# P kept in fp32 for 7 of 16 groups of the filter stages, and the order of the steps where they end

## The chip, the cores and the metric

The kernel runs on one core of a Trainium2 chip. The metric is device time in microseconds (us) of one execution. A core has five engines with instruction queues of their own: PE (TensorE, the matmul array, whose weight loads the profile shows as PEld), DVE (VectorE), ACT (ScalarE), POOL (GpSimd) and SP (SyncE, which here only issues DMAs).

## The reference

Four layers on x of 2048 tokens by 640 channels: a spectral filter, a token mixer, and the same two again.

```python
def _A_ref(x, w_r, w_i):
    X = jnp.fft.rfft2(x, axes=(-2, -1))
    X = X * (w_r + 1j * w_i)
    return jnp.fft.irfft2(X, (S, D), axes=(-2, -1))

def _B_ref(x, w1, b1, w2, b2):
    h = _layernorm(x, axis=-1)
    u = _gelu(jnp.einsum("bsd,sf->bdf", h, w1) + b1)
    y = jnp.einsum("bdf,fs->bds", u, w2) + b2
    return y.transpose(0, 2, 1)

x = A_x
x = x + _A_ref(_layernorm(x, axis=-1), A_w_r, A_w_i)
x = x + _B_ref(_layernorm(x, axis=-1), B_w1, B_b1, B_w2, B_b2)
x = x + _A_ref(_layernorm(x, axis=-1), A_w_r, A_w_i)
x = x + _B_ref(_layernorm(x, axis=-1), B_w1, B_b1, B_w2, B_b2)
```

## The kernel before

The Fourier transforms are done as matrix products with tables. Nearly every operand of a product is held as two fp16 numbers, a high part and the remainder (names in h and l), and a product is three matmuls: high by high, high by low, low by high.

A filter layer has three parts. A first one transforms the tokens of each of 16 tiles (s1h, s1l). The second one, `a1`, is what the change is about and is called the filter stage here: it goes over 16 groups of rows of the spectrum. The third, `a2`, transforms back over the channels (products of Y with the table tDi), copies the result out as eh and el, transforms over the tokens (products with tIM) and adds to x. The first filter stage lies at 59.3 to 119.8 us of the profile, the second at 536.9 to 599.1.

The steps of one group in `a1`, with the names of the schedule:

- d: PE multiplies s1h, s1l and a stack of leftovers (stk) with the table tD; the result P lies in PSUM.
- ph: ACT copies P, scaled, into fp16 (ph). pl: DVE takes P minus ph into fp16 (pl).
- sA and sB: PE multiplies P with the table tS2, in two halves. The array is used as four quadrants of 64x64; a half is 12 matmuls, three rounds over the quadrants. The second half waits for an ACT instruction that is itself tied to the end of the first half (marked `&` in the schedule; for group 0 it is DVE's small copy `between`).
- ta and tb: DVE multiplies the result with the filter weights w. sa and sb: POOL adds and subtracts them.
- xh, xl, uh, ul: ACT and POOL split the product into fp16 parts, and ACT repeats some columns.
- i: PE transforms back (tI2). Yh, Yl: ACT and DVE copy the result out in two fp16 parts.

Four PSUM slots are shared by the steps (`@` gives the slot). The order of all steps is written out by hand in `STEPS`, one string for each of the two filter stages, and each engine keeps it. Steps that begin with e belong to neighbouring work: ea4 to ea7 are ACT's part of splitting the first weight tile of the mixer (`wsplit`, four pieces of wh), ev10 is DVE's computing of the scale cxe that eh needs, ev4 DVE's computing of the scale s that the weight pieces need. They stand at the end of the first stage's string.

```python
for op in STEPS[not first].split():
    if op[0] == "e":
        scale(op)
        continue
    do(op)
```

In `a2`, iteration i does the product of Y for tile i (`id_mm`), then el and the tIM product of tile i - 1, and near its end eh of tile i.

Of the kernel before, what the change touches and what calls it, by code (L numbers as in the profile page):

```python
# [59 lines left out]
TS = 4096.0  # L60
# [30 lines left out]
class Layers:  # L91
# [226 lines left out]
    def a0_open(self, first=False):  # L318
        nc, A = self.nc, self.A
        p = self.pS1 = self.push("S1", side=self.sp)  # L320
        self.s1h = p.tile([128, 80, 2, 16, 4], F16, name=f"s1h{self.n}")
        self.s1l = p.tile([128, 80, 2, 16, 4], F16, name=f"s1l{self.n}")
        self.tD = p.tile([128, 20, 161], F16, name=f"tD{self.n}")
        self.tS2 = p.tile([128, 2, 2, 4, 128], F16, name=f"tS2{self.n}")
        self.tI2 = p.tile([128, 2, 2, 2, 128], F16, name=f"tI2{self.n}")
        p = self.pT = self.push("a0", side=self.sp)
        if first:
            self.tM = [p.tile([128, 4, 128], F32, name=f"tM{q}_{self.n}") for q in range(4)]
        else:
            self.tM = [p.tile([128, 4, 2, 128], F16, name=f"tM{q}_{self.n}") for q in range(4)]  # L330
# [149 lines left out]
    def a1(self, first):  # L480
# [190 lines left out]
        ps = dstage(0, slots[0])  # L671
        if not first:
            self.wsplit(0, (0,), hi=False)
        pp[0] = tuple(self.t(p, [128, 2, 322], F16, a, 3) for a in ("ph", "pl"))
        sc = PQS / (S1S * TS)
        for q in range(2):
            a, b, c = ps[:, q, :NL], pp[0][0][:, q, :NL], pp[0][1][:, q, :NL]
            T.activation(b, a, AF.Copy, scale=sc)
            V.scalar_tensor_tensor(c, a, sc, b, op0=ALU.mult, op1=ALU.subtract)

        def acted(ins, gs):

            for g in map(int, gs.split(",") if gs else ()):
                follow(ins, half[g])
                half[g] = ins

        def do(op):
# [101 lines left out]
    def a2(self, li):  # L789
# [69 lines left out]
        for i in range(NJ + 5):  # L859
# [1266 lines left out]
def _shape_tables():  # L2126
# [66 lines left out]
```

## Time and profile before

| | |
|---|---|
| median of 3 runs | 976.7 us (975.47 to 977.51) |
| the profiled execution | 974.83 us, of which its span from first to last instruction is 973.1 us |
| PE busy | 932.0 us, 96% of the span |
| DVE busy | 754.3 us, 78% |
| ACT busy | 564.6 us, 58% |
| POOL busy | 293.4 us, 30% |
| chain that ended last | PE 55%, DVE 21%, ACT 8%, POOL 7% |

The profile is of one execution. Busy shares are over the whole span; the mixer stages, which fill most of it, keep PE at work with the other engines partly idle, and the filter stages are short. Ends of matmuls are modelled and overlap each other, so PE's busy time is not time at its peak. The chain that ended last is followed back from the last instruction to what released each step.

### The profile page before, as it was taken

How to read it: one execution, taken by the hardware profiler on the slowest of the kernel's cores; microseconds unless marked ns; L12 is line 12 of the kernel's file. 1: busy time of each engine (PE TensorE's matmuls, PEld its weight loads, DVE VectorE, ACT ScalarE, POOL GpSimd, SP SyncE). 2: the span in 40 equal slices, each digit the busy share in tenths (PEclk: the TensorE clock that was granted, in tenths of full speed). 3: DMA queues.
4: the chain of work that ended last, by engine and by line, in shares of the span. 5: the costliest groups of instructions: out<-in, count | busy, mean ns of one | idle time of the engine just before them, and what ended most of it. 6: DMA issues, size and time to landing. Idle time of an engine off the chain costs nothing.

```text
span 973.1 us, 22470 instructions
## 1 busy us (share of the span) xinstructions
PE 932.0 (96%) x9009; PEld 691.0 (71%) x9009; DVE 754.3 (78%) x1407; ACT 564.6 (58%) x869; POOL 293.4 (30%) x496
## 2 busy tenths in 40 slices
PE   4889899999999999999999998999999999999998
PEld 3768777677767677677776776776777777777776
DVE  7989989999788956566667897889645445998885
ACT  5857869885667774455544476784433335455431
POOL 6949867311111112222222595771000000000000
PEclk9999999999999999999999999999999999999999
DMA  7856377654876776664232663764555447655411
GB/s 254 290 159 175 107 235 243 224 174 161 317 272 228 278 251 205 229 187 130 97 108 74 192 183 104 247 221 162 169 156 170 142 132 289 205 189 177 139 52 49
DMA packets 68108, 179.42 MB, mean 184 GB/s; under 512 B 8010, under 2 KB 15332, under 8 KB 68004
## 3 DMA queue, kind: packets, MB, share of 16 engines
q1 hardware_dynamic: 60820, 151.63, 48.5%
q0 software_dynamic: 7184, 26.36, 7.4%
q8 instruction: 70, 1.15, 0.5%
q14 instruction: 34, 0.28, 0.1%
HBM read 130.39 MB, written 47.58 MB: 183 GB/s over the span
## 4 chain that ended last, share of the span: by engine, by line
PE 55%; DVE 21%; ACT 8%; POOL 7%; issue 5%; DMA 3%; SPq 0%; ACTq 0%; DVEq 0%; POOLq 0%
PE ps L83 55%; DVE f L83 4%; DVE wl L83 3%; POOL eo L83 3%; DVE st L83 3%; DVE s1l L83 2%; ACT wh L83 2%; ACT z L83 1%; DMA xt<-x 1%; ACT junk L83 1%; DVE xt L83 1%; DVE Yl L83 1%; POOL xl L83 1%; POOL ta L83 1%; DVE tb L83 1%
## 5 line engine op out<-in xcount | busy, mean ns | idle before, releaser
L83 PEld LDWEIGHTS <-wh 128*128 128x128 f16 x2298 | 222.4, 98 | 88.8 <-issue 2.1
L83 PE MATMUL ps<-u,wh 128*128 128x320 f16 x1242 | 228.6, 299 | 0.0
L83 PEld LDWEIGHTS <-wl 128*128 128x128 f16 x1626 | 158.8, 98 | 66.0 <-DVE wl L83 3.0
L83 PE MATMUL ps<-u,wl 128*128 128x320 f16 x826 | 182.1, 299 | 1.0 <-DVE wl L83 0.5
L83 PEld LDWEIGHTS <-wo 128*128 128x128 f16 x924 | 90.3, 98 | 35.1
L83 POOL TENSOR_TENSOR r<-v,mh 128x1 f32<-128x1 f32 x64 | 39.4, 615 | 148.0 <-DVE nm L83 138.4
L83 PE MATMUL ps<-tDi,Yh 128*128 128x322 f16 x320 | 71.3, 300 | 1.5 <-ACT Yh L83 1.5
L83 DVE TENSOR_TENSOR f<-eo 128x256 f32<-128x256 f32 (+1 forms) x124 | 39.1, 368 | 37.0 <-POOL eo L83 36.3
L83 ACT ACTIVATE junk<-raw 128x896 bf16<-128x896 f32 (+1 forms) x60 | 59.5, 991 | 13.3 <-DMA raw<-w 12.5
L83 POOL TENSOR_TENSOR xt<-xt,ec 128x320 f32<-128x320 f32 x64 | 53.3, 853 | 29.9 <-DVE xt L83 29.8
L83 ACT ACTIVATE z<-xt,nb,r 128x640 f32<-128x640 f32 x31 | 28.5, 919 | 54.2 <-POOL z L83 45.1
L83 DVE BATCH_NORM_STATS2 st<-xt 128x6 f32<-128x320 f32 x126 | 55.2, 479 | 5.2 <-DMA xt<-x 4.6
L83 PE MATMUL ps<-u,wo 128*128 128x320 f16 x420 | 58.8, 299 | 0.0
L83 PE MATMUL ps<-tM,f 128*128 128x128 f32 x160 | 39.1, 419 | 19.4 <-DVE f L83 19.4
L83 POOL TENSOR_TENSOR eo<-z 128x320 f32<-128x320 f32 x60 | 52.3, 892 | 17.0 <-ACT z L83 15.2
L83 PE MATMUL ps<-tDi,Yl 128*128 128x322 f16 x192 | 55.7, 299 | 1.4 <-DVE Yl L83 1.4
L83 DVE SCALAR_TENSOR_TENSOR wl<-raw,s,wh 128x896 f16<-128x896 f32 (+2 forms) x43 | 47.9, 1122 | 7.3 <-ACT wh L83 7.3
L83 PEld LDWEIGHTS ps<-tM,f 128*128 128x128 f32 x160 | 33.4, 300 | 24.9 <-DVE f L83 24.5
L83 POOL TENSOR_TENSOR xl<-ta,xh 128x642 f16<-128x642 f32 (+2 forms) x34 | 45.5, 1346 | 5.0 <-ACT xh L83 4.9
L83 ACT ACTIVATE wh<-raw,s 128x896 f16<-128x896 f32 (+2 forms) x46 | 43.6, 987 | 3.1 <-DVE s L83 1.8
L83 DVE SCALAR_TENSOR_TENSOR u<-f,su,u 128x1280 f16<-128x1280 f32 (+2 forms) x26 | 25.5, 996 | 25.4 <-ACT u L83 25.2
L83 POOL MEMSET wl<- 64x256 f16 x2 | 0.6, 306 | 146.5 <-DMA wl<-w2A 146.5
(257 smaller groups left out, 2237.6 us busy)
## 6 DMA issues: line engine op xcount, KB each, us to landing
xt<-x SPq DMA_DIRECT2D x79, 320.0 KB
raw<-w SPq DMA_DIRECT2D x32, 512.0 KB
w<-w SPq DMA_DIRECT2D x48, 321.0 KB
x<-xt SPq DMA_DIRECT2D x47, 320.0 KB
raw<-w SPq DMA_DIRECT2D x32, 448.0 KB
raw<-w2z SPq DMA_DIRECT2D x32, 448.0 KB
out<-xt SPq DMA_DIRECT2D x15, 320.0 KB
w1S<-wl POOLq DMA_DIRECT2D x9, 512.0 KB, 6.4
```

The lines of the kernel that those rows point to most:

```text
L83: i = f(*a, **k)
```

## The change

For groups 0, 1, 2, 12, 13, 14 and 15 (`WHOLE`), in both filter stages, P is copied by ACT into one fp32 tile pf, and no pl is made. The two s halves of such a group multiply pf with a new fp32 table tS1, four matmuls a half instead of twelve. tS1 (1024 fp32 numbers a partition) is loaded with the other tables. In the first stage's string, ev10 comes ahead of ev4, and ea4 to ea7 go; ACT's four wh pieces are issued in `a2` instead, one behind eh of each of the tiles 0 to 3. In the second stage's string some of the last steps change places (Yl7 comes earlier, and the second half of group 15 is tied to xh13 instead of ul12).

```diff
 STEPS = '''
-    Yh14 Yl12 xl15b i15a@0 uh15 ul15 Yl14 i15b@3 Yh15a Yh15b Yl15a Yl15b ev4 ev10 ea4 ea5 ea6 ea7
+    Yh14 Yl12 xl15b i15a@0 uh15 ul15 Yl14 i15b@3 Yh15a Yh15b Yl15a Yl15b ev10 ev4
...
-    sB14 pl15 sa13 i9@1 xh12 ta14 ul10 sb13 uh12 i8@3 Yh7 tb14 xl12 Yh9 sb14 sA15@0 xh13 sa14 Yl9 uh13 ul12&15 xl13
-    xh14 sB15 Yl7 ul11 i10@1 uh14 Yh8 ta15a xl14 i11@2 tb15a Yh10 ta15b ul13 sa15a tb15b ul14 Yl8 Yh11 i13@0 sb15a
+    sB14 sa13 i9@1 xh12 ta14 ul10 sb13 uh12 i8@3 Yh7 tb14 Yl7 xl12 sA15@0 xh13&15 Yh9 sb14 uh13 sa14 Yl9 ul12 xl13
+    xh14 sB15 ul11 i10@1 uh14 Yh8 ta15a xl14 i11@2 tb15a Yh10 ta15b ul13 sa15a tb15b ul14 Yl8 Yh11 i13@0 sb15a
...
+WHOLE = 0, 1, 2, 12, 13, 14, 15
...
+        self.tS1 = p.tile([128, 2, 4, 128], F32, name=f"tS1{self.n}")
...
         nc.sync.dma_start(self.tI2, A["tI2"])
+        nc.sync.dma_start(self.tS1, A["tS1"])
...
-        def psplit(ps):
+        def psplit(ps, g):
+            sc = PQS / (S1S * TS)
+            if g in WHOLE:
+                pf = self.t(p, [128, 2, 322], F32, "pf", 3)
+                yield T.activation(pf[:, :, :NL], ps[:, :, :NL], AF.Copy, scale=sc)
+                yield pf
...
         def s2half(g, ps, x, half):
 
             out = []
+            if g in WHOLE:
+                for R, C in ((0, 0), (0, 1), (1, 1), (1, 0)):
+                    ri, q = R ^ half, R ^ C
+                    out.append(mm(
+                        ps[HALF[C], ri, :NL], self.tS1[HALF[R], 1 if g == 0 else 0, 2 * ri + q, HALF[C]], x[HALF[R], q, :NL],
+                        start=half == 0, stop=half == 1,
+                    ))
+                return out[0], out[-1]
...
             if has[0]:
                 eo[i] = ehigh(pd[i])
+                if first and i < 4:
+                    c = i ^ 2
+                    self.wsplit(0, (c // 2,), lo=False, part=slice(c % 2 * 4, c % 2 * 4 + 4))
```

What this moves on the engines is seen best in the order of their instructions (names carry buffer numbers, which differ between the two kernels). On PE, at the first groups of the first stage, the rows before are these, from the small product of eye and xb to the first matmul with pl; each matmul has a weight load of its own.

```order
L83 MATMUL ps_908<-eye,xb 128x16
L83 LDWEIGHTS tS_197
L83 MATMUL ps_908<-ph_1026,tS_197 64x321
L83 LDWEIGHTS tS_197
...
L83 LDWEIGHTS tS_197
L83 MATMUL ps_908<-pl_1027,tS_197 64x321
```

And these are the rows of the change at that place, with group 0's eight matmuls ahead of it, up to the next d block; fp32 matmuls load their weights themselves, without a row.

```order
L84 MATMUL ps_909<-pf_967,tS_199 64x321 x8
L84 MATMUL ps_910<-eye,xb 128x16
L84 MATMUL ps_910<-pf_1025,tS_199 64x321 x4
L84 LDWEIGHTS s1h_194
L84 MATMUL ps_911<-tD_196,s1h_194 64x160
```

Twelve weight loads and twelve matmuls have become four rows of pf. On DVE, at the same place, before:

```order
L83 SCALAR_TENSOR_TENSOR pl_966<-ps_907,ph_965 128x321 x2
L83 COPY between_911<-between_911 128x1
L83 TENSOR_REDUCE xm<-ps_908 16x1
L83 COPY xb<-xm 16x128
L83 SCALAR_TENSOR_TENSOR pl_1027<-ps_908,ph_1026 128x2x321
L83 TENSOR_SCALAR xqq<-ps_908 128x16
```

and in the change:

```order
L84 COPY between_913<-between_913 128x1
L84 TENSOR_REDUCE xm<-ps_910 16x1
L84 COPY xb<-xm 16x128
L84 TENSOR_SCALAR xqq<-ps_910 128x16
L84 TENSOR_SCALAR qi_232_1053<-xqq 128x16
```

The rows of pl are gone and nothing took their place. On ACT, at the seam between the first filter stage and `a2`, the rows before, behind the last Yh:

```order
L83 ACTIVATE wh_1346<-raw_1342,s_72 128x512 x2
L83 ACTIVATE wh_1346<-raw_1344,s_72 128x512 x2
L83 ACTIVATE eh_2878<-ps_2861,cxe 128x644
L83 ACTIVATE eh_2906<-ps_2880,cxe 128x644
L83 ACTIVATE ec_2937<-ps_2899 128x322
```

and in the change:

```order
L84 ACTIVATE eh_2749<-ps_2732,cxe 128x644
L84 ACTIVATE wh_1293<-raw_1291,s_72 128x512
L84 ACTIVATE eh_2778<-ps_2752,cxe 128x644
L84 ACTIVATE wh_1293<-raw_1291,s_72 128x512
L84 ACTIVATE ec_2810<-ps_2771 128x322
L84 ACTIVATE eh_2818<-ps_2784,cxe 128x644
L84 ACTIVATE wh_1293<-raw_1289,s_72 128x512
```

The four pieces of wh have moved from ahead of the first eh to places behind each of the first four.

## Rows read from the trace of the kernel before

**Rows 1.** Windows, both filter stages: from:to length, busy us (instructions), PEclk, DMA, GB/s

```profile
core 0: us, PE busy (x) PEld busy (x) DVE busy (x) ACT busy (x) POOL busy (x), PEclk, DMA share, GB/s
59.30:119.80 60.50, 56.30 (x1511) 46.47 (x1511) 54.72 (x93) 43.80 (x91) 49.03 (x59) 1.00 0.51 148
536.90:599.10 62.20, 55.90 (x1507) 45.88 (x1508) 55.96 (x89) 41.26 (x84) 49.32 (x64) 1.00 0.63 187
```

**Rows 2.** Waits of PE, first filter stage: us in total, times, longest us

```profile
PE ps L83 <- DVE Yl L83: 1.0, 2, 0.6
PE ps L83 <- DVE pl L83: 0.9, 2, 0.6
PE ps L83 <- DVE ta L83: 0.6, 2, 0.4
PE ps L83 <- DVE between L83: 0.3, 1, 0.3
PE ps L83 <- DVE tb L83: 0.2, 1, 0.2
```

**Rows 3.** Waits of PE, second filter stage

```profile
PE ps L83 <- ACT xl L83: 1.7, 1, 1.7
PE ps L83 <- DVE Yl L83: 1.5, 2, 1.2
...
PE ps L83 <- DVE pl L83: 0.7, 2, 0.4
```

**Rows 4.** Groups of instructions by shape, DVE, first filter stage

```profile
L83 DVE SCALAR_TENSOR_TENSOR Yl<-ps,Yh 128x384 f16<-128x384 f32 x30 | 14.7, 544 | 0.0
L83 DVE SCALAR_TENSOR_TENSOR ta<-ps,sx,w 128x642 f32<-128x642 f32 x15 | 13.2, 879 | 0.9 <-issue 0.4 <-POOL xl L83 0.3 <-PE ps L83 0.2
L83 DVE SCALAR_TENSOR_TENSOR tb<-ps,sx,w 128x642 f32<-128x642 f32 x15 | 13.2, 878 | 0.4 <-PE ps L83 0.2 <-DMA w<-w 0.2
L83 DVE SCALAR_TENSOR_TENSOR pl<-ps,ph 128x642 f16<-128x642 f32 x15 | 12.3, 817 | 0.0
```

**Rows 5.** Timeline of PE, 72 to 82 us: start us, length us, what

```profile
72.42 0.33 PE L83 MATMUL ps<-tD,s1h 128*64 128x160 f16 x4
...
73.69 0.33 PE L83 MATMUL ps<-ph,tS 64*64 64x321 f16 x4
73.85 0.31 PE L83 MATMUL ps<-pl,tS 64*64 64x321 f16 x4
73.98 0.44 PE L83 MATMUL ps<-ph,tS 64*64 64x321 f16 x8
...
74.63 0.33 PE L83 MATMUL ps<-tD,s1h 128*64 128x160 f16 x4
...
80.53 0.29 PE L83 MATMUL ps<-tI,xh 64*128 64x128 f16 x4
...
81.64 0.33 PE L83 MATMUL ps<-ph,tS 64*64 64x321 f16 x4
```

**Rows 6.** Timeline of PE, fp32 matmuls ahead of and in the first stage

```profile
57.56 0.94 PE L83 MATMUL ps<-tM,f 128*128 128x128 f32 x7
...
62.80 0.39 PE L83 MATMUL ps<-eye,xq 128*16 128x128 f32 x2
```

**Rows 7.** Groups by shape, PE, 57.75 to 58.33 us

```profile
L83 PE MATMUL ps<-tM,f 128*128 128x128 f32 x7 | 0.9, 275 | 0.0
```

**Rows 8.** Timeline of ACT, DVE and PE behind the first filter stage

```profile
121.43 2.56 ACT L83 ACTIVATE wh<-raw,s 128x512 f16<-128x512 f32 x4 [1.77 <-DVE s L83]
...
122.49 0.17 DVE L83 TENSOR_REDUCE cxe<-xof 128x1 f32<-128x16 f32 x1
124.70 0.89 DVE L83 SCALAR_TENSOR_TENSOR el<-ps,cxe,eh 128x644 fp32r<-128x644 f32 x1 [2.04 <-ACT eh L83]
...
124.42 0.30 PE L83 MATMUL ps<-tDi,Yl 128*128 128x322 f16 x1
...
125.65 0.42 PE L83 MATMUL ps<-el,tIM 128*128 128x322 f32 x1 [0.51 <-DVE el L83]
```

**Rows 9.** Timeline of SP, one load of a table

```profile
24.95 0.45 SPq L339 DMA_DIRECT2D tI<-tI  x1
```

More of the change, by code (lines that the diff above doesn't have):

```diff
@@ L27 @@
 STEPS = '''
-    d1@1 ep8 ph1 sA0@0 ev8 pl1 sB0 ep9 sA1@1 ev9 d2@2 tb0 d3@3 ta0 ph2&1 pl2 sb0 sB1 sa0 ea1 sA2@2 tb1 ph3 d4@0 xh0&2
+    d1@1 ep8 ph1 sA0@0 ev8 sB0 ep9 sA1@1 ev9 d2@2 tb0 d3@3 ta0 ph2&1 sb0 sB1 sa0 ea1 sA2@2 tb1 ph3 d4@0 xh0&2
     pl3 xl0 ta1 sB2 ph4 sA3@3 ta2 d5@1 sa1 ul0&3 pl4 uh0 sb1 sB3 tb2 ph5 sA4@0 tb3 d6@2 sb2 xh1&4 pl5 sa2 sB4 ta3 xl1
@@ L32 @@
     Yh2 Yl1 xl5 ul3 sA8@1 ph10 Yl2 d11@3 xh6&8 sb7 pl10 uh4 ul4 xl6 sB8 ea2 sA9@2 ta8 i4@0 ph11&9 sa7 tb8 uh3 sB9 Yh4
-    pl11 sA10@1 sb8 tb9 d12@3 sa8 xh7&10 Yl4 ul5 ul6 xl7 uh5 sB10 uh6 ph12 ta9 i3@0 pl12 sa9 sA11@2 ta10 xh8 sb9 d13@3
-    Yh3&11 tb10 xl8 xh9 Yl3 sB11 sA12@1 sa10 ta11 i5@0 uh9&12 sb10 ph13 tb11 ea3 xl9 sB12 pl13 d14@2 Yh5 tb12 sb11
-    d15@3 ta12 sa11 ph14 ul7 pl14 xh10 sa12 sA13@1 Yl5 sb12 i6@2 ph15&13 xl10 ul8 pl15 uh7 sB13 xh11 sA14@0 tb13 uh11
+    pl11 sA10@1 sb8 tb9 d12@3 sa8 xh7&10 Yl4 ul5 ul6 xl7 uh5 sB10 uh6 ph12 ta9 i3@0 sa9 sA11@2 ta10 xh8 sb9 d13@3
+    Yh3&11 tb10 xl8 xh9 Yl3 sB11 sA12@1 sa10 ta11 i5@0 uh9&12 sb10 ph13 tb11 ea3 xl9 sB12 d14@2 Yh5 tb12 sb11
+    d15@3 ta12 sa11 ph14 ul7 xh10 sa12 sA13@1 Yl5 sb12 i6@2 ph15&13 xl10 ul8 uh7 sB13 xh11 sA14@0 tb13 uh11
     i7@3 Yh6 xl11 ta13 ul9&14 uh8 ep1 sB14 xh12 Yl6 sa13 sA15@1 Yh7 tb14 xl12 i8@2 ul10 uh10&15 ta14 ul11 uh12 sB15
@@ L38 @@
     tb15a i13@0 Yh10 ta15b tb15b sb15a Yl11 ul14 i12@1 Yh13 sa15a Yl10 sb15b xh15a sa15b i14@2 xh15b Yh12 xl15a Yl13
-    Yh14 Yl12 xl15b i15a@0 uh15 ul15 Yl14 i15b@3 Yh15a Yh15b Yl15a Yl15b ev4 ev10 ea4 ea5 ea6 ea7
+    Yh14 Yl12 xl15b i15a@0 uh15 ul15 Yl14 i15b@3 Yh15a Yh15b Yl15a Yl15b ev10 ev4
 ''', '''
-    d1@1 sA0@0 ph1 sB0 pl1 tb0 sA1@1 d2@2 ta0 sa0 d3@0 ph2&1 sb0 pl2 sB1 ph3 sA2@2 tb1 d4@3 xh0&2 pl3 ta1 xl0 sB2 ph4
+    d1@1 sA0@0 ph1 sB0 tb0 sA1@1 d2@2 ta0 sa0 d3@0 ph2&1 sb0 sB1 ph3 sA2@2 tb1 d4@3 xh0&2 pl3 ta1 xl0 sB2 ph4
     sA3@0 tb2 d5@1 sb1 ul0&3 pl4 sa1 ta2 sB3 ph5 sA4@3 xh1 ta3 d6@2 sb2 uh0&4 pl5 sa2 sB4 tb3 xl1 ph6 sA5@1 tb4 d7@0
@@ L45 @@
     Yl1 sB8 sa7 ph10 sA9@2 tb8 xh6 d11@0 ul2 pl10 uh6&9 xl6 sB9 ta8 ph11 sA10@1 sb7 ul5 pl11 i2@3 uh4&10 sb8 tb9 d13@0
-    sa8 Yh2 ta9 xh7 Yl2 sB10 sa9 sA11@2 ph13 tb10 xl7 d12@3 ul4&11 xh8 pl13 ul6 sb9 sB11 ta10 ph12 i4@0 xl8 uh5 tb11
-    i6@1 pl12 Yh4 sa10 ta11 xh9 i5@3 sb10 Yh6 Yl4 xl9 sA12@2 ul7 Yh5 Yl6 d14@0 sb11 uh7&12 xh10 Yl5 sa11 sB12 uh10 uh8
-    sA13@1 ph14 xl10 tb12 d15@3 xh11&13 pl14 xl11 sB13 ta12 ph15 sA14@0 ul8 ta13 i7@2 sa12 uh9&14 uh11 tb13 ul9 sb12
-    sB14 pl15 sa13 i9@1 xh12 ta14 ul10 sb13 uh12 i8@3 Yh7 tb14 xl12 Yh9 sb14 sA15@0 xh13 sa14 Yl9 uh13 ul12&15 xl13
-    xh14 sB15 Yl7 ul11 i10@1 uh14 Yh8 ta15a xl14 i11@2 tb15a Yh10 ta15b ul13 sa15a tb15b ul14 Yl8 Yh11 i13@0 sb15a
+    sa8 Yh2 ta9 xh7 Yl2 sB10 sa9 sA11@2 ph13 tb10 xl7 d12@3 ul4&11 xh8 ul6 sb9 sB11 ta10 ph12 i4@0 xl8 uh5 tb11
+    i6@1 Yh4 sa10 ta11 xh9 i5@3 sb10 Yh6 Yl4 xl9 sA12@2 ul7 Yh5 Yl6 d14@0 sb11 uh7&12 xh10 Yl5 sa11 sB12 uh10 uh8
+    sA13@1 ph14 xl10 tb12 d15@3 xh11&13 xl11 sB13 ta12 ph15 sA14@0 ul8 ta13 i7@2 sa12 uh9&14 uh11 tb13 ul9 sb12
+    sB14 sa13 i9@1 xh12 ta14 ul10 sb13 uh12 i8@3 Yh7 tb14 Yl7 xl12 sA15@0 xh13&15 Yh9 sb14 uh13 sa14 Yl9 ul12 xl13
+    xh14 sB15 ul11 i10@1 uh14 Yh8 ta15a xl14 i11@2 tb15a Yh10 ta15b ul13 sa15a tb15b ul14 Yl8 Yh11 i13@0 sb15a
     sa15b Yl10 xh15a sb15b i12@3 Yh13 xl15a Yl11 i14@1 xh15b uh15 Yh12 Yl13 xl15b i15a@2 ul15 Yh14 Yl12 i15b@0 Yh15a
@@ L575, in dstage @@
             return ps
-        def psplit(ps):
+        def psplit(ps, g):
[4 more added lines that the diff above has]
+                yield pf
             ph = self.t(p, [128, 2, 322], F16, "ph", 3)
             pl = self.t(p, [128, 2, 322], F16, "pl", 3)
-            sc = PQS / (S1S * TS)
             yield T.activation(ph[:, :, :NL], ps[:, :, :NL], AF.Copy, scale=sc)
@@ L673, in a1 @@
             self.wsplit(0, (0,), hi=False)
-        pp[0] = tuple(self.t(p, [128, 2, 322], F16, a, 3) for a in ("ph", "pl"))
-        sc = PQS / (S1S * TS)
+        pp[0] = self.t(p, [128, 2, 322], F32, "pf", 3)
         for q in range(2):
-            a, b, c = ps[:, q, :NL], pp[0][0][:, q, :NL], pp[0][1][:, q, :NL]
-            T.activation(b, a, AF.Copy, scale=sc)
-            V.scalar_tensor_tensor(c, a, sc, b, op0=ALU.mult, op1=ALU.subtract)
+            T.activation(pp[0][:, q, :NL], ps[:, q, :NL], AF.Copy, scale=PQS / (S1S * TS))
         def acted(ins, gs):
@@ L694, in do @@
             if name == "d":
-                dst[g] = psplit(dstage(g, ps))
+                dst[g] = psplit(dstage(g, ps), g)
             elif name == "ph":
                 acted(next(dst[g]), f)
+                if g in WHOLE:
+                    pp[g] = next(dst.pop(g))
             elif name == "pl":
@@ L2139, in _shape_tables @@
     t["tS2"] = np.stack(_split16(s2.transpose(2, 0, 1, 3)), axis=1)
+    t["tS1"] = (s2.transpose(2, 0, 1, 3) * TS).astype(np.float32)
     t["tI2"] = np.stack(_split16(i2.transpose(2, 0, 1, 3)), axis=1)
```

## The prediction

> **What bounds the kernel now.** [...] The list of PE's waits shows how little PE idles in the first stage, 3.0 us over five causes, all of them DVE [rows 2]; in the second its longest wait is one of 1.7 us for ACT's xl, and two DVE entries make 2.2 us [rows 3].
>
> PE's share must not be read from its busy time, because modelled ends overlap. I take start times from the timeline instead: one group's d block runs from 72.42 to 73.69 (1.27 us), two adjacent s halves, which is one group's worth, from 73.69 to 74.63 (0.94 us), an i block from 80.53 to 81.64 (1.11 us) [rows 5]. So 3.32 us a group with the changes between kinds of block, 53.1 us for 16 groups. Of 60.5 us, PE leaves 7.4 us unused, of 62.2 us 9.1 us, 16.5 us in both; the named waits are part of it, the rest is start-up and blocks that begin a little late.
>
> DVE needs per group one pl (0.817 us), ta (0.879), tb (0.878) and two Yl (0.544 each) [rows 4]: 3.66 us, more than PE's 3.32. Both engines are thus near the bound. What the change takes from DVE it must not pay for twice on PE.
>
> **The change, part by part.** *DVE.* In seven groups of each stage pl goes. 7 x 0.817 is 5.7 us of DVE per stage [rows 4]. That is worth at most what DVE holds PE up for: 3.0 us in the first stage [rows 2] and the 2.2 us of the two DVE entries in the second [rows 3], 5.2 us together; less if PE becomes the later one.
>
> *ACT.* pf replaces ph with as many instructions and as many elements, only the output is four bytes wide instead of two. No row here has that very form, and I take no difference: the input and the count stay.
>
> *PE.* This is the large term. Before, a group has 24 matmuls of 64x64 weights and 321 columns. In the rows four of them, one for each quadrant of the array, start together and the next four follow 0.13 to 0.16 us later (73.69, 73.85, 73.98) [rows 5]: 6 x 0.137 = 0.82 us plus the change of kind. After, a group has 8 fp32 matmuls, but the profile shows each fp32 matmul as two passes, each with its own weight load (the one matmul of eye and xq stands there as x2 [rows 6]). Seven passes of 128 columns take from 57.56 to 0.94 us later, the last one is 0.275 long [rows 6, 7], so (0.94 - 0.275) / 6 = 0.111 us from one to the next, and that with weight loads of 128 columns hidden. The two of eye and xq, 0.39 us together, give the same size. A pass thus costs 0.87 ns a column against 0.137 / 321 = 0.43 ns of fp16, and a pass over 321 columns 0.28 us. [...]
>
> Eight matmuls are 16 passes. What they cost depends on how many run side by side, which no row shows for fp32 in quadrants. Bounds: all four quadrants side by side through both passes, 16 / 4 x 0.28 = 1.1 us a group, +0.3 us; nothing side by side, 16 x 0.28 = 4.5 us, +3.7 us. I take a value between, from the order of the instructions. A matmul's second pass needs the same quadrant as its first, and stands directly behind it, ahead of the next quadrant's first pass. In the fp16 rows a quadrant's second use begins only 0.13 us after its first, when that has streamed through (73.85 to 73.98 [rows 5]). If PE starts passes in program order, the second pass holds everything behind it back for 0.28 us; then it and the next quadrant's first pass go together. Two at a time, then: eight matmuls in a row take 9 passes, 2.5 us, which is +1.7 us a group, 7 x 1.7 = 11.9 us a stage, 23.8 us in both.
>
> [...]
>
> What covers PE's added 23.8 us is the 16.5 us that it leaves unused, and not all of it: part is the chain at the start (the first s half, then DVE's small copy, then the second half) and the last Y copies before the next stage, which stay. If none stays, the two stages cost 2 x (53.1 + 11.9) = 130.0 us against 122.7, +7.3; if all stays, +23.8. I take half, 8.2 us: 138.2, **+15.5 us**. DVE's 5.7 us per stage then buy nothing, since PE is late everywhere.
>
> *The seam after the first stage.* ACT now does four pieces of wh in 2.56 us from 121.43 and only then the first copy eh; DVE's cxe, without which eh has no scale, is not issued until 122.49; el waits 2.04 us for eh and starts at 124.70; PE has ended the second Y product (its last start is 124.42, so 0.14 later) and stands until el is there, at 125.65 [rows 8]. After, the five instructions for cxe come right behind the last Yl, six small ones earlier, and eh stands ahead of the first wh piece. The two products are 16 matmuls of 0.137 us each, so the first is through 2.2 us before 124.56, at 122.36. Then eh can follow at about 122.6, when cxe is ready too, and el is done near 124.4, before PE wants it. PE's stand from 124.56 to 125.65 goes: **-1.1 us**. The wh pieces then lie one behind each eh. A piece is 0.64 us (a quarter of 2.56) in an iteration whose products alone are 2.2 us on PE, and wl, which needs it, comes after el on DVE; if that cover failed, the piece would hold up an eh by 0.64 us four times, +2.6 us, the upper bound of this term.
>
> *The table.* tS1 is one more load per filter stage, issued on SP right behind the load of tI, whose issue at 24.95 takes 0.45 us [rows 9]. Its 512 KB (1024 fp32 a partition) come 34 us ahead of the stage that uses them; x loads run three tiles ahead, so I count nothing; uncovered it would be one issue, 0.45 us, twice. The second time, at the end of the first mixer, one weight load on SP stands behind it instead of ahead, and one of ACT's sums of squares moves a step later with it; the weights are loaded four tiles ahead there, which covers that.
>
> *Order of the last steps in the second stage.* The s half of group 15 is tied to an ACT copy that comes earlier (xh13 instead of ul12): of PE's 1.7 us wait for xl [rows 3] it can remove what xl12 adds. With PE late I count nothing; at most 1.7 us less.
>
> **Sum.** +15.5 - 1.1 = +14.4 us. The profiled execution took 974.8 us (span 973.1), so 989.2 by its time; the median of the runs shown is 976.7, 1.9 above it, so **991 us**.
>
> **Rivals.** *All four quadrants side by side (the faster side).* PE pays 2 x 7 x 0.3 = 4.2 us. DVE's 5.2 us of stalls on PE go, and the seam's 1.1: -2.1 us, 974.6; with PE's other waits unchanged and no stall removed it would be +3.1, with the 1.7 us of xl removed too -3.8. For it: fp16 quadrants do run four at a time [rows 5]. Against: it needs a first pass to start while an earlier second pass still stands in line. It decides from a cost of about 1.2 us a group downwards: 0.38 x 14 is 5.3 us, as much as the DVE stalls. The gap from 73.69 to 73.85, wider than 0.137, says that even fp16 blocks pay something at their start.
>
> *One pass at a time.* +3.7 us x 14 = 51.2 us, of which half of the 16.5 us idle covers 8.3: +43 - 1.1, about 1018.6 us. For it: fp32 rows here all use the whole width or height of the array, none shows two passes together. Against: fp16 quadrants are independent, and only the element type changes.
>
> *Two at a time but well covered.* The seven groups are the first three and the last four, where PE's idle lies. If nearly all 16.5 us are used: +7.3 - 1.1 = +6.2, 983 us; if nearly nothing, +22.7, 999. That is the range of the likeliest case itself: 983 to 999.
>
> **How the numbers follow.** Two at a time 0.45 (991, 983 to 999); four at a time 0.33 (974.6, 973 to 977, now and then 980); one at a time 0.10 (1019); the rest 0.12, mostly something between two and four at a time (977 to 985). Within 0.2% (about 2 us) is what a measurement of this kernel can't tell from no change. Of the four-at-a-time case I put 0.22 below that and 0.09 within; with a little from the rest: faster 0.24, same 0.13, slower 0.63. Both signs hold much of the chance, so the range runs from the lower end of the second case to the upper end of the first, 972 to 1000, which leaves out one at a time and the tails, 0.2.
>
> **What would show it.** In the profile of the changed kernel, a fp32 group's eight matmuls should take some 2.5 us from first to last start, a first pass starting together with the second pass of the matmul ahead of it, and d and i blocks around them should be late; DVE should show waits for PE in the groups 12 to 15 where it showed none. The seam should show el beginning near 123.5 us plus the stage's shift and no PE wait for it. I am wrong if the eight matmuls take about 1.1 us (faster or same), if they take about 4.5, or if they take 2.5 and the stages still grow by less than 3 us each, which would mean that PE's unused 16.5 us were all usable.

## The result and the profile after

The changed kernel takes 980.92 us (median of 5 runs, 980.06 to 983.12), the kernel before 976.7 us (5 runs, 974.99 to 977.51): ratio 1.0043, 95% interval 1.0023 to 1.0062. It is slower by 4.2 us, where the forecast was 14.4 us. The profiled execution took 980.86 us, span 979.1.

The windows of the two filter stages after, from PE's first d block to the last i block, with the columns of [rows 1]:

```profile
60.79:122.06 61.27, 58.00 (x1455) 45.41 (x1455) 49.10 (x85) 43.27 (x90) 49.12 (x61) 1.00 0.53 157
540.80:604.03 63.23, 56.99 (x1388) 44.37 (x1383) 48.85 (x78) 40.36 (x82) 49.46 (x64) 0.97 0.55 164
```

Against [rows 1] the stages are 0.8 and 1.0 us longer, and DVE has 5.6 and 7.1 us less to do. Of the 6.0 us between the two profiled executions (980.86 against 974.83) 4.2 lie in neither stage's length, and what the stages lose is far less than the forecast's 15.5 us in both. The profile before stands at a granted clock of 1.00 from 51.5 us to its end; the changed kernel's has three falls of TensorE's granted clock to 0.50 or 0.51 (last section), of which, by the estimate given there, the two outside the stages can make up to about 3 of the 4.2 us, and the one inside the second stage as much as that stage's 1.0 us. The medians, 4.2 us apart, are the safer difference.

PE's timeline of the first fp32 groups (start us, length us):

```profile
66.76 0.77 PE L84 MATMUL ps<-pf,tS 64*64 64x321 f32 x8
...
70.60 1.31 PE L84 MATMUL ps<-pf,tS 64*64 64x321 f32 x16
71.84 0.33 PE L84 MATMUL ps<-tD,s1h 128*64 128x160 f16 x4
```

Two adjacent halves, one group's worth, start at 70.60 and the next block at 71.84: 1.24 us, against 0.94 in [rows 5]. Other fp32 groups show the same (106.55 to 107.79, 548.54 to 549.78). The windows of that tile alone count how many passes are in flight in the half at 66.76 (us, PE busy and in brackets the count):

```profile
66.80:67.06 0.26, 0.26 (x4) 0.17 (x8) 0.00 (x0) 1.00 0.46 113
67.09:67.11 0.02, 0.02 (x8) 0.00 (x0) 0.00 (x0) 1.00 0.48 103
```

Four passes run together for the first 0.3 us, and just behind it the four second passes have joined them. All four quadrants work side by side.

PE's waits in the first stage, which answer to [rows 2] (us in total, times, longest):

```profile
PE ps L84 <- DVE Yl L84: 1.0, 2, 0.6
PE ps L84 <- issue: 0.5, 1, 0.5
PE ps L84 <- DVE between L84: 0.3, 1, 0.3
PE ps L84 <- DVE ta L84: 0.2, 1, 0.2
```

And in the second, which answer to [rows 3]:

```profile
PE ps L84 <- DVE Yl L84: 2.2, 2, 1.2
PE ps L84 <- DMA stk<-rest: 1.8, 1, 1.8
PE ps L84 <- ACT xh L84: 0.9, 1, 0.9
PE ps L84 <- ACT Yh L84: 0.7, 1, 0.7
```

The waits for pl are gone, as is the one of 1.7 us for xl. New are one of 1.8 us for the load of stk, which has nothing to do with P, one for xh, and in the first stage one of 0.5 us put to issue (waiting for nothing that the profile shows), at the first use of stk.

The seam behind the first stage, timeline of ACT, DVE and PE:

```profile
124.81 0.80 ACT L84 ACTIVATE eh<-ps,cxe 128x644 fp32r<-128x644 f32 x1 [2.90 <-PE ps L84]
125.50 0.71 ACT L84 ACTIVATE wh<-raw,s 128x512 f16<-128x512 f32 x1
...
123.74 0.17 DVE L84 TENSOR_REDUCE cxe<-xof 128x1 f32<-128x16 f32 x1
...
125.72 0.89 DVE L84 SCALAR_TENSOR_TENSOR el<-ps,cxe,eh 128x644 fp32r<-128x644 f32 x1 [0.81 <-ACT eh L84]
...
126.67 0.30 PE L84 MATMUL ps<-tDi,Yl 128*128 128x322 f16 x1
126.69 0.42 PE L84 MATMUL ps<-eh,tIM 128*128 128x322 f32 x1
126.95 0.31 PE L84 MATMUL ps<-el,tIM 128*128 128x322 f32 x1
```

eh now follows its product, the piece of wh comes behind it, and PE goes on to el without the stand of [rows 8].

### The profile page after: what moved, and what is told of

Same layout as the page of the kernel before. It is cut to its first block, busy times and chain, and to the rows that moved or that the text cites. A ratio compares the mean times of both kernels' runs of the same rounds, so it can differ in the third digit from the quotient of the medians.

```text
span 979.1 us, 22224 instructions
## 1 busy us (share of the span) xinstructions
PE 936.5 (96%) x8897; PEld 689.5 (70%) x8897; DVE 744.9 (76%) x1391; ACT 564.2 (58%) x869; POOL 293.6 (30%) x496
## 3 DMA queue, kind: packets, MB, share of 16 engines
q8 instruction: 70, 1.15, 0.5%
## 4 chain that ended last, share of the span: by engine, by line
PE 58%; DVE 19%; ACT 8%; POOL 6%; issue 4%; DMA 4%; SPq 0%; ACTq 0%; POOLq 0%; DVEq 0%
PE ps L84 58%; DVE f L84 3%; DVE wl L84 3%; DVE st L84 3%; POOL eo L84 2%; DVE s1l L84 2%; DMA xt<-x 2%; ACT junk L84 1%; DMA raw<-w 1%; ACT z L84 1%; ACT wh L84 1%; DVE Yl L84 1%; DVE xt L84 1%; POOL ta L84 1%; POOL xt L84 1%
## 5 line engine op out<-in xcount | busy, mean ns | idle before, releaser
L84 PE MATMUL ps<-u,wo 128*128 128x320 f16 x420 | 58.8, 299 | 0.0
```

The costliest lines, as they stand in the source:

```text
L84: i = f(*a, **k)
```

## The experiments

Each kernel was timed beside the kernel before on the same chip, in four groups: e1 to e4, e5 to e8, e9 to e12, e13 to e16. Differences are against the median of before in the same group (976.94, 977.05, 976.7 and 976.65 us).

**The parts alone.** The first theory was read off the two traces: the second stage, and loads that land late, make the loss. e1 and e2 limit fp32 to one stage, each with that stage's order and table load; e1 has the seam. `WHOLE` becomes one set for each stage:

```diff
-WHOLE = 0, 1, 2, 12, 13, 14, 15
+WHOLES = (0, 1, 2, 12, 13, 14, 15), ()
...
 def a1(self, first):
+    WHOLE = WHOLES[not first]
```

e3 is the kernel before with the tile and both loads, e4 with the seam's two edits:

```diff
+        nc.sync.dma_start(self.tS1, A["tS1"])
```

```diff
-    ... Yl15b ev4 ev10 ea4 ea5 ea6 ea7
+    ... Yl15b ev10 ev4
...
                 eo[i] = ehigh(pd[i])
+                if first and i < 4:
+                    c = i ^ 2
+                    self.wsplit(0, (c // 2,), lo=False, part=slice(c % 2 * 4, c % 2 * 4 + 4))
```

> The change in the first filter stage alone: fp32 P and table for its seven groups, its new order of the last steps and the pieces of wh behind eh; the second stage as before, without the second load of tS1. Theory A (what the first stage loses or gains is swallowed later, by PE's wait of 0.8 us for DVE's sqb at 276 us): within 0.5 us of the kernel before, ratio 1.000. Theory B (the 1.0 us by which the end of the first mixer's a2 stands later in the changed kernel is carried to the end): +1.0 us, ratio 1.001. Theory C (the fp32 stage as such pays 7 x 0.30 us, and nothing hides it): +2.1 less the seam's 1.0, ratio 1.001.

> The change in the second filter stage alone, with its load of tS1; the first stage and the seam behind it as before. Theory A (all of the loss is made in the second stage, in its fp32 groups and behind them, and at the end of the first mixer where the new load stands): nearly the whole of the change, +4 us, ratio 1.004. Theory B (each stage pays its half): +2 us, ratio 1.002. [...]

> The kernel before with the tile tS1 and both its loads added and not used; nothing else changed. Theory A (the longer waits for raw near 408 us, 1.3 us, and for stk near 546 us, 1.4 us, come from the added load and from the place that it takes in the order of the loads): +1.3 to +2.7 us, ratio 1.0013 to 1.0028. Theory B (the load is hidden, and those waits come from the fp32 stage or differ from one execution to the next): within 0.5 us, ratio 1.000.

> The kernel before with the new order of the last steps and the pieces of wh behind eh after the first filter stage, all in fp16, without tS1. PE's stand of 1.1 us for el at the seam should be gone from the profile. Theory A (what is gained there is lost again in a wait further on, at the latest at 276 us): within 0.5 us of the kernel before, ratio 1.000. Theory B (it is carried to the end): -1.1 us, ratio 0.9989.

| | us (runs) | to before | ratio, 95% |
|---|---|---|---|
| e1, first stage | 981.63 (7) | +4.7 | 1.0047, 1.0028 to 1.0065 |
| e2, second stage | 977.87 (12) | +0.9 | 1.0005, 0.9989 to 1.0021 |
| e3, loads | 977.20 (12) | +0.3 | 1.0004, 0.9991 to 1.0017 |
| e4, seam | 975.77 (12) | -1.2 | 0.9984, 0.9972 to 0.9997 |

Theory A failed where it was firmest: the first stage alone makes the whole loss, the second next to none. The seam gives what the prediction gave it, and is carried to the end; e4 beats both kernels, the one before by 1.2 us. e3's 0.3 us is no clear difference. But e1's own profile shows its first stage hardly longer than before (60.74 to 121.63, 60.9 us against 60.5); most of its time is lost between 128 and 600 us, where its program is that of the kernel before.

**Which part of the first stage.** e5 is the changed kernel with fp16 in the first stage, e6 has groups 12 to 15 of the first stage alone in fp32 (the first diff, against e1), e7 groups 0 to 2, e8 is e1 with its table loaded later (the second diff):

```diff
-WHOLES = (0, 1, 2, 12, 13, 14, 15), ()
+WHOLES = (12, 13, 14, 15), ()
```

```diff
         for a in scans:
             a()
+        nc.sync.dma_start(self.tS1, A["tS1"])
         self.pin = False
```

> The changed kernel with the first filter stage back in fp16 (its seven pl on DVE again, six matmul passes), and all the rest of the change kept: the seam, fp32 in the second stage, tS1 loaded for the second stage alone. Theory A, formed from the runs so far (the loss is fp32 in the first stage or its table's load, the rest adds up to about nothing): -0.7 us against the kernel before (the seam's -1.2 and the second stage's +0.5), ratio 0.9993, and some 5 us below the changed kernel. Theory B (the parts do not add; any fp32 stage together with the seam costs): +4 us, ratio 1.004.

> The first stage alone changed as in the run of the first stage alone, but with groups 12, 13, 14 and 15 in fp32 only; groups 0 to 2 in fp16 with their pl on DVE; tS1 loaded for the first stage, and the seam. Theory A (a cost by group on PE, so that four of seven groups pay four sevenths): +1.9 us against the kernel before, ratio 1.002. Theory B (what costs is the start of the stage, its first three groups or its table's load there): -1 us if it is the groups, +4 if it is the load. Theory C (what costs is the end of the stage, where PE's added passes hold up the last Y copies): +4 us, ratio 1.004.

> The counterpart: groups 0, 1 and 2 of the first stage in fp32, groups 12 to 15 in fp16; tS1 loaded for the first stage, and the seam. Theory A (a cost by group): three sevenths of 5.6 us less the seam's 1.2, +1.2 us, ratio 1.001. Theory B (the start of the stage or its load): +4 us, ratio 1.004. Theory C (the end of the stage): -1 us, ratio 0.999.

> The run of the first stage alone (seven groups in fp32, the seam) with one edit: the load of tS1 is issued behind the last x tile and not behind the load of tI, eleven loads later. Theory A (the 512 KB of tS1 push back the x tiles that the stretch before the stage waits for, which stood 1.4 us late at 56 us in that run): 1.4 us below that run, about +3 us against the kernel before, ratio 1.003. Theory B (the place of the load is of no account): the same as that run, +4.5 us, ratio 1.0047.

| | us (runs) | to before | ratio, 95% |
|---|---|---|---|
| e5 | 977.81 (12) | +0.8 | 1.0004, 0.9984 to 1.0023 |
| e6, 4 groups | 981.52 (5) | +4.5 | 1.0053, 1.0033 to 1.0073 |
| e7, 3 groups | 983.43 (6) | +6.4 | 1.0073, 1.0051 to 1.0096 |
| e8, late table | 978.96 (12) | +1.9 | 1.0028, 1.0010 to 1.0046 |

e5's +0.8 is far from theory B's +4, and its interval holds theory A's -0.7. Three groups cost no less than seven, so this is no price by group, nor the start or the end of the stage. What e1, e6 and e7 share is the table's early load, without which e8 still loses 1.9 us, and that PE has fewer instructions from the first stage on: by the counts of the profiles seven fp32 groups leave out some 110, four some 65, three some 48. The view of the DMA queues has a queue for instructions that nothing in the kernel issues. Its row for the kernel before from 535.5 to 538 us (packets, MB, share of 16 engines):

```profile
q8 instruction: 1, 0.02, 2.4%
```

One packet of 16 KB in a moment of little other traffic; 2.4% of 16 engines' 2.5 us is 0.96 us of one of them. From 538 to 545 us, when the leftovers stk go out to DRAM and come back, the kernel before has no such row. The changed kernel, from 541 to 545 us:

```profile
q8 instruction: 1, 0.02, 1.5%
```

There it falls among them. Over the whole span there are 70 such packets, 1.15 MB, for the 18,018 PE instructions that the profile counts (9009 matmuls and as many weight loads): 257 instructions, about 64 bytes each, to a packet. That it is PE's instructions that these packets carry is read from this count, and tested next.

**The instruction count.** Theory F was tested without any fp32: e9 and e10 add instructions at the start of the kernel before, where PE stands idle, and change no other engine's program. e11 and e12 give e1 and the changed kernel back the 110 that the first stage's fp32 groups leave out; the other 110, which the changed kernel's second stage leaves out, stay out in e12.

```diff
         self.setup()
+        self.pin = True
+        for k in range(4):
+            b = self.big()
+            for _ in range(n // 4 + (k < n % 4)):
+                self.PE.matmul(b[:, 0, :1], self.ones, self.ones[:, :1], start=True, stop=True)
+        self.pin = False
```

where n stands for the number written in each kernel: 73, 128, 55 and 55. Each matmul is two instructions, weight load and matmul.

> The kernel before with 146 PE instructions added in front of everything (73 one-column matmuls of a tile of ones, each with its weight load, at the very start, where PE stands idle until 11.6 us); nothing else differs, on no engine. Theory F: PE's instructions come in by transfers of 16 KB, 256 instructions each, which show in the trace as an instruction queue; one takes 0.9 to 2.0 us of one of the 16 DMA engines, and a load that meets it lands that much later. Seven fp32 groups take 110 instructions out of PE's stream, so all later transfers fall elsewhere: in the runs with fp32 in the first stage one falls among the loads of stk at the start of the second stage (543.8 us), where the kernel before has it 7 us earlier in an idle moment (536.4). 146 instructions more shift them as 110 fewer do (256 to a transfer), so theory F expects +2 to +5 us, ratio 1.002 to 1.005. Rival A (fp32 itself costs): no change, ratio 1.000.

> The same with 256 PE instructions added at the start, one whole transfer of 16 KB, so that the later transfers fall where they fell. Theory F: no change, ratio 1.000. Rival G (any PE instruction at the start costs, by the clock or by the first loads): as much as the run with 146.

> The run of the first stage alone (seven groups in fp32, the seam, tS1's first load) with 110 PE instructions added at the very start, as many as its fp32 groups leave out, so that behind the first stage the instruction transfers fall as in the kernel before. Theory F: the 4 to 5 us go, to within 1.5 us of the kernel before, ratio 0.999 to 1.0015. Rival A (fp32 in the first stage costs by itself): as without them, ratio 1.0047.

> The changed kernel, whole, with 110 PE instructions added at the very start, so that from the end of the first stage to the middle of the second the instruction transfers fall as in the kernel before. Theory F: within 1.5 us of the kernel before, ratio 0.999 to 1.0015, at or below it if the seam's 1.2 us come through. Rival A: as the changed kernel, ratio 1.004.

| | us (runs) | to before | ratio, 95% |
|---|---|---|---|
| e9, before + 146 | 980.54 (12) | +3.8 | 1.0034, 1.0017 to 1.0051 |
| e10, before + 256 | 976.59 (12) | -0.1 | 0.9997, 0.9985 to 1.0009 |
| e11, e1 + 110 | 978.72 (12) | +2.0 | 1.0027, 1.0008 to 1.0047 |
| e12, changed + 110 | 978.79 (12) | +2.1 | 1.0024, 1.0008 to 1.0039 |

The fp16 kernel becomes as slow as the changed one by 146 idle PE instructions, and stays as it was with 256. That is theory F's sign. The other half held in part: 2.7 us (e1 to e11) and 2.1 us (the changed kernel to e12) go, 2 us stay, where theory F allowed 1.5 at most. By the intervals each of these two gains is uncertain by some 2.5 us.

The trace of e9 shows the changed kernel's own waits in the first mixer. ACT's sums of squares there need a load of weights (raw), and PE then waits for wl. PE's wait, 400 to 415 us, in the changed kernel:

```profile
PE ps L84 <- DVE wl L84: 1.4, 1, 1.4
```

in e9, and in the kernel before:

```profile
PE ps L83 <- DVE wl L83: 1.4, 1, 1.4
```

```profile
PE ps L83 <- DVE wl L83: 0.5, 1, 0.5
```

It comes behind this wait of ACT, in e9 and then before (timeline of ACT; in the changed kernel the same wait is 1.93 us):

```profile
406.42 0.95 ACT L83 ACTIVATE junk<-raw 128x896 bf16<-128x896 f32 x1 [2.27 <-DMA raw<-w]
```

```profile
402.99 0.95 ACT L83 ACTIVATE junk<-raw 128x896 bf16<-128x896 f32 x1 [0.41 <-DMA raw<-w]
```

In both the changed kernel and e9 an instruction packet is under way just ahead of the issue of that load on SP, at 398.33 and at 400.17 us; the rows of the queue from 396.4 to 398.4 us in the changed kernel, and from 398.2 to 400.2 us in e9:

```profile
q8 instruction: 1, 0.02, 3.0%
```

```profile
q8 instruction: 1, 0.02, 3.1%
```

The kernel before has no such row from 392 to 405 us, and e10, with 256 more, has none there either and waits 0.49 us.

**The rest.** e13 is e12 with the table's first load moved as in e8; e16 is e11 with that load moved. e14 and e15 are the kernel before with n = 96 and n = 32.

> The changed kernel with 110 PE instructions added at the start, as in the run before of this kind, and tS1's first load issued behind the last x tile. Theory L (the 2 us that were left come from the early load of 512 KB): 1.3 us or more below that run, ratio to the kernel before 0.999 to 1.001. Rival P (they are the fp32 passes, 0.30 us for each of 14 groups, less what DVE gains): as that run, ratio 1.0024.

> The kernel before with 192 PE instructions added at the start, nothing else. It shifts the instruction transfers as 64 instructions fewer do, which is what four fp32 groups leave out (65). Theory F: +2 to +5 us, as the run with groups 12 to 15 in fp32 (+4.5 us); ratio 1.002 to 1.005. Rival (the loss in that run was those four groups at the end of the stage): no change, 1.000.

> The kernel before with 64 PE instructions added at the start, nothing else: a fourth place of the instruction transfers. Theory F says only that it may differ from the kernel before in either direction. If it is slower as well, the kernel before stands at a favourable place, and any change that alters PE's count before 600 us is likely to lose 2 to 4 us; if it is equal or faster, it does not.

> The first stage alone in fp32 (seven groups) with the seam, PE's instruction count restored at the start and tS1's load behind the last x tile. Theory L: the seam's gain of 1.2 us comes through, less at most 0.5 us for the passes: ratio 0.9985 to 0.9995. Rival P: seven passes of 0.30 us, 2.1 us less 1.2, ratio 1.001 or more.

| | us (runs) | to before | ratio, 95% |
|---|---|---|---|
| e13, e12 + late table | 978.70 (12) | +2.1 | 1.0021, 1.0007 to 1.0035 |
| e14, before + 192 | 982.10 (6) | +5.5 | 1.0063, 1.0045 to 1.0082 |
| e15, before + 64 | 981.97 (9) | +5.3 | 1.0048, 1.0028 to 1.0067 |
| e16, e11 + late table | 977.31 (12) | +0.7 | 1.0005, 0.9994 to 1.0015 |

All three counts that are not 256 (64, 146 and 192) are 3.8 to 5.5 us slower: the kernel before stands at a favourable place. e14 repeats e6's +4.5 without fp32.

The padded kernels are no exact copy of what the change does to the count, though: they shift the transfers from the start, the change only from its first fp32 group on. DVE's step ta in the first stage, before and in e9:

```profile
76.24 0.88 DVE L83 SCALAR_TENSOR_TENSOR ta<-ps,sx,w 128x642 f32<-128x642 f32 x1
```

```profile
78.43 0.88 DVE L83 SCALAR_TENSOR_TENSOR ta<-ps,sx,w 128x642 f32<-128x642 f32 x1
```

The same step begins at 78.56 us in e14, at 78.64 in e15, and at 75.92 in e10. In these profiles 2.2 to 2.4 us of the loss thus lie ahead of this step, where the changed kernel's count is only beginning to differ (its first three fp32 groups lie at 64.6 to 71.8 us). Not all of it need be the count: e4, with the count of before, begins the step at 77.58, and in e9 TensorE's granted clock stands at 0.50 from 55.5 to 58.8 us, as it does for a while in the changed kernel's profile. e11, e12, e13 and e16 carry such an early shift too.

Another of the places where e15 loses is again the load of stk (PE's timeline, before and then e15):

```profile
543.94 0.26 PE L83 MATMUL ps<-tD,stk 96*64 96x160 f16 x2 [0.42 <-DMA stk<-rest]
```

```profile
547.60 0.26 PE L83 MATMUL ps<-tD,stk 96*64 96x160 f16 x2 [2.23 <-DMA stk<-rest]
```

and e15's row of the instruction queue in the half us from 544.0:

```profile
q8 instruction: 1, 0.02, 14.3%
```

The moved load gained 2.8 us from e1 to e8, 1.4 from e11 to e16 and nothing from e12 to e13 (2.09 and 2.05), each uncertain by 2 us or more: theory L is not shown, and the whole change keeps its 2 us without the early load, as rival P expected. e16 decides nothing between them: its 1.0005 lies between L's 0.9995 and P's 1.001, and its interval reaches both. e8 and e16 are a third pair that differs by the count alone: restoring it gains 1.3 us there, after 2.7 and 2.1. The three gains average 2.0 us, by the intervals uncertain by some 1.3 us.

## Why the prediction was off, point by point

**fp32 on PE: the step that failed.** "If PE starts passes in program order, the second pass holds everything behind it back for 0.28 us; ... Two at a time, then": 2.5 us a group and +11.9 us a stage. Measured are 1.24 us a group (70.60 to 71.84), +0.30, the +0.3 of the rival with four quadrants side by side. The premise was wrong: the first passes of four quadrants start together, then the four second passes (four in flight from 66.80 to 67.06 us, eight from 67.09). With that step corrected, the prediction's own sum is that of the rival, from -2.1 to +3.1 us, that is 974.6 to 979.8 us by the medians. The measured 980.9 lies 1.1 us above even its worse end.

**What DVE gives back.** The 5.2 us of stalls on DVE were not all to be had. The waits for pl went, those for Yl stayed (1.0 and 2.2 us, above), so the stages pay a part of PE's 2.1 us each (an estimate, 7 x 0.30). By the runs the first stage's fp32 costs +1.8 us (e16's 0.66 against the -1.17 of e4) and the second's +0.9 to +1.9 (e2; e5 against e4), each uncertain by 1.5 to 2.3 us. These prices are not the passes' alone: e16 has its 110 instructions too many ahead of the first stage, and in e2 and e5 the 110 that the second stage leaves out stay out behind it. The rival's worse end, +3.1 with no stall removed, was the near one.

**The half that is covered.** 8.2 of 16.5 us was a choice, not a reading, and was not needed, since PE's work grew by about 4.2 us (14 x 0.30) and not by 23.8.

**The seam.** Right in mechanism and size: -1.1 forecast, -1.2 measured by itself (e4), and PE's wait for el gone.

**The table.** Nothing was counted, +0.3 us was measured with both loads unused (e3, 1.3 us either way). Whether its early place costs something once the stage uses it stays open.

**The last steps of the second stage.** In the profile the 1.7 us for xl went, and 0.9 for xh and 0.7 more for Yl came; costing it at nothing was right by this sum.

**What no step had: PE's instruction count.** Seam -1.2, fp32 +1.8 and about +1.4 make +2.0, which agrees with e12 and e13 (+2.1 each), within uncertainties as large as the terms. The other 2.1 us of the 4.2 go when the 110 instructions that the first stage leaves out of PE's stream are given back (2.0 us on average of three pairs, uncertain by some 1.3). That the count alone moves the time is shown by e9, e10, e14 and e15, which change nothing else. That the transfers of PE's instructions are the cause is shown in so far as the effect vanishes at 256, about the 257 counted to a packet; a period of 128 would fit the four counts as well. What the 2 us are that stay is not shown: the price of the fp32 passes, the early shift of the padded kernels, and the second stage's 110 instructions, which no run gives back, were not separated. How a transfer costs the time was only read from the traces, in two forms: a load that meets one lands later (PE's wait for stk is 2.23 us in e15 against 0.42, ACT's for raw 2.27 in e9 against 0.41), and PE itself stands with nothing to wait for that the profile shows, until 2.20 to 2.45 us behind the start of one (below). How much each contributes was not separated.

**Sign and rivals.** Slower was right, for about 2 us perhaps by a price that a rival had, and for about 2 us by one that nobody had; that the sign came true was luck, since the step that gave it was wrong. The prediction's own sign of being wrong came true, eight matmuls in about 1.1 us; what it tied to that, faster or the same, did not. The forecast's main term was too large by 19.6 us (23.8 against 4.2 of PE work).

## What to carry to other kernels

When a kernel is tuned to a few tenths of a per cent, add idle instructions to the engine with the longest program (here PE, where 64, 146 and 192 cost 3.8 to 5.5 us and 256 cost nothing, -0.1) before believing a small loss or gain: a change that leaves out instructions is judged more safely with the count restored, or over several counts. fp32 matmuls in quadrants cost little over three fp16 rounds (1.24 us a group here against 0.94), and here they did not pay: DVE was relieved, but the waits for its Yl stayed. And a reading of where a trace of before and one of after drift apart names the places where time is lost, not the edit that lost it: here it named the second stage, and the runs named the first.

## What the runs showed of the hardware

While the kernel before runs, 70 packets of 16 KB come in the instruction queue, one for every 257 of PE's recorded instructions. About 256 to a packet agrees with the counts that cost and the one that does not (+256: -0.1 us; +64, +146, +192: +5.3, +3.8, +5.5 us). Here the place of the packets is worth 0.4 to 0.6%.

PE can also stand behind such a packet with no wait that the profile shows. In e14 a packet is under way between 581.5 and 582.5 us (its row of the queue), and PE's next stop, in its timeline, is put down to issue:

```profile
q8 instruction: 1, 0.02, 5.8%
```

```profile
584.08 0.26 PE L83 MATMUL ps<-tD,s1l 128*64 128x160 f16 x2 [1.25 <-issue]
```

The same stands in e2 at 573.83 and 579.30 us, behind packets in the windows from 571 to 572 and from 576.7 to 577.2:

```profile
573.83 0.23 PE L84 MATMUL ps<-tI,xl 64*128 64x128 f16 x2 [0.72 <-issue]
...
579.30 0.23 PE L84 MATMUL ps<-tD,stk 98*64 98x161 f16 x1 [1.01 <-issue]
```

The profiles of all these kernels have 23 stops of PE of more than 0.25 us that are put down to issue. Five stand at the first use of stk in the first stage, 4.4 us or more behind a packet. The other 18, all but one in the second stage, end 2.20 to 2.45 us behind the start of a packet, each of them. Most packets pass without a stop, and e3, whose PE instructions are those of the kernel before, has one too (0.55 us), so the place of a packet alone does not make it. Nor are the stops the whole loss: e14's two make 1.5 of its 5.5 us, and e15 has none.

The kernel before has no such stop in its filter stages, so part of what the second stage's fp32 costs may be this and not its passes.

TensorE's granted clock fell from 1.00 to 0.50 or 0.51 three times in the changed kernel's profile between 51 and 978 us: just ahead of the first filter stage, near the end of the second, and behind it (windows; PEclk is the third number from the end):

```profile
57.10:60.50 3.40, 3.40 (x14) 2.27 (x13) 2.26 (x6) 2.04 (x5) 0.00 (x0) 0.50 0.30 105
...
593.00:596.40 3.40, 3.40 (x70) 3.40 (x68) 3.21 (x8) 2.07 (x5) 3.10 (x6) 0.50 0.00 0
...
603.20:606.60 3.40, 3.40 (x14) 1.95 (x13) 0.00 (x0) 0.00 (x0) 0.00 (x0) 0.51 0.92 317
```

Each costs at most some 1.7 us, an estimate: half of its 3.40 us, at half the granted clock. It is no mark of fp32: e4, all in fp16, shows one as well, behind a stretch in which PE was busy for 1.44 of 3.5 us:

```profile
598.00:601.50 3.50, 1.44 (x30) 0.76 (x24) 3.13 (x9) 1.97 (x5) 0.66 (x7) 1.00 0.50 142
601.60:604.90 3.30, 3.30 (x14) 1.89 (x13) 0.00 (x0) 0.00 (x0) 0.00 (x0) 0.50 0.04 11
```

The profiled execution before has none there. Runs of one kernel differ in it: the mean granted clock of the 26 executions of the kernel before that were timed beside e13 to e16 lies between 0.977 and 0.998. This is part of why a profile of one execution could not be read to 1 us.
